# Weight sums of the value product made in two column pieces, and copies of projected V shared by two engines

## Chip, cores and metric

The kernel runs on one core of one Trainium2 chip. The metric is the device time of one execution in microseconds, the median over several runs; lower is better.

## What is computed

The reference is a linear attention followed by a gated feed-forward layer, for 8 batches, 8 heads, 1024 positions and a head width of 64:

```python
k_proj = np.einsum('ks,bhsd->bhkd', E, k)          # 64 projected keys per head
v_proj = np.einsum('ks,bhsd->bhkd', F, v)
scores = scale * np.matmul(q, k_proj.transpose(0, 1, 3, 2))
attn = softmax(scores)                              # over the 64 projected keys
x = np.matmul(attn, v_proj)                         # laid out as 8192 tokens x 512
gate = 1.0 / (1.0 + np.exp(-(x @ w_gate)))          # 512 x 1536
out = (gate * (x @ w_val)) @ w_out                  # w_val 512 x 1536, w_out 1536 x 512
```

## The kernel before

The tokens are worked in blocks of 512 columns, two blocks for each batch, sixteen in all. For a block, the gate product (G), the value product (V), the gating and the output product follow each other, and the attention of a later batch is laid between them. All operations are added to one plan in program order (class `Plan`); each engine runs its own operations in that order, and a wait is put in front of an operation for each semaphore value that its inputs, or the buffers that it overwrites, still need. So the order in which the program calls its helpers is the order of every engine's queue. Lists called `todo` give the slots of that order, and `put(i, fn)` or `on(u, j, fn)` adds a piece of work behind slot i, or behind slot 11 + 9u + j.

Block 0 is worked plainly: `mstep(0, m)` multiplies the m-th of twelve 128-column chunks of both weights, and `gate` (L1126) reads the V bank on VectorE. From block 1 on, V is made with Strassen's method in Winograd's form: seven products of half size in place of eight. A unit K is a block and a "quad" q (K = 3 x block + q); a quad is two chunks of the first half of the 1536 columns with the two that lie 768 columns on. `v_pieces` (L1497) issues the seven products of a unit in five steps, in the order p1, p26, p57, p4, p3, with the four gate steps `g_step` of the unit between them. They accumulate in two PSUM banks, called a and c in the code. ScalarE takes snapshots of bank a (`v_snap`, L1465), VectorE adds bank c to a snapshot (`v_add`, L1468), and `hidden` (L1444) multiplies with the gate. The first step p57 starts a new sum in bank c, so it waits for the `v_add(0)` of p26, which reads bank c.

The products take sums of the inputs and sums of the weights. The sums of the inputs, S1 to S4, are made per block by `xs_sums` (L1406, VectorE, 128 x 512 bf16 each). The sums of the weights, T1 to T4, are made once, by `vt_sums` (L1372 to L1394, VectorE, 128 x 1536 bf16 each): T3 = B22 - B12, T2 = T3 + B11, T4 = B21 - T2, and T1 = B12 - B11, which overwrites B12. T2, T3 and T4 go to the tensor `vT`, T1 stays in `wV`. Each sum covers all three quads. T2 is used by p26, T1 and T3 by p57, T4 by p4.

Around the start of block 1 (K = 3, its first unit) VectorE's queue reads: gate of chunk 10 of block 0; T3; S1; S2; gate of chunk 11; T2; T1; S3; S4; T4; `v_add(0)`; `hidden`. The gate of chunk 11 frees the PSUM bank that p26 takes as its bank c. In unit K = 4 the function `v_alone` (L811) turns the projected keys of batch 1 and projects its values into one PSUM bank; `keep_v` (L529) copies four quarters (64 x 256) of that bank to `vpD`, all four on ScalarE; ScalarE's next item is `v_snap(2)`, for which the PE's next product p4 waits. The four copies read one bank, and the plan lets operations on one bank follow one another.

The loads come through two queues. POOL issues (L282), in this order, the second batch's Q, K and V, then the output weights `wO` behind the first two DMA transposes of Q (SP, L745), then K, V and Q of batch 2. The output products of block 0 (`oproj`, L1146) are the first to use `wO`.

Of the kernel before, what the change touches and what calls it, by code (L numbers as in the profile page):

```python
# [12 lines left out]
P = 128  # L13
# [5 lines left out]
DFF = 1536  # L19
# [99 lines left out]
def bass_linformer_attn__then__ffn_glu_sigmoid_kernel(  # L119
# [11 lines left out]
    B = q.shape[0]  # L131
# [6 lines left out]
    with contextlib.ExitStack() as es:  # L138

        def sbuf(name, shape, dtype):  # L140
            return es.enter_context(nc.sbuf_tensor(name, shape, dtype))


        vT = sbuf("vT", [P, 3, 2, DFF // 2], BF16)
# [61 lines left out]
        wV = sbuf("wV", [P, NI, DFF], BF16)  # L206
# [49 lines left out]
        def mm(b, o, lhsT, rhs, r, start=True, stop=True, tp=None, tr=False, read=False):  # L256
            kw = {"skip_group_check": True} if read else {}
            if tp is not None:
                kw["tile_position"] = tp
            if tr:  # L260
                kw["is_transpose"] = True
            else:
                kw["start"], kw["stop"] = start, stop
            return add("PE", lambda e: e.matmul(o, lhsT, rhs, **kw), r=r, x=[("bank", b)])  # L264

        def act(o, i, r, w, b=None, func=AF.Copy, scale=1.0):
            x = [] if b is None else [("bank", b)]
            return add("ACT", lambda e: e.activation(o, i, func, scale=scale), r=r, w=w, x=x)  # L268

        def dve(fn, r, w, b=None):  # L270
            x = [] if b is None else [("bank", b)]
            return add("DVE", fn, r=r, w=w, x=x)
# [224 lines left out]
        def pairs(R):  # L497
            return slice(0, NR) if R is None else slice(2 * R, 2 * R + 2)

        def both(R):  # L500
            return (0, 1) if R is None else (R,)

        def project(n, w, bks, c0, R=None):
            src = KV[n][:, :, :].rearrange("p (r h) (t d) -> p h t r d", h=2, t=NT)
            width = 256 if R is None else 128
            for t in range(NT):
                for h in range(2):
                    mm(
                        bks[h],
                        bank[bks[h]][64 * h : 64 * h + 64, c0 : c0 + width],  # L510
                        EFT[:, t, 64 * w : 64 * w + 64],
                        src[:, h, t, pairs(R), :],
                        [("KV", n, x) for x in both(R)] + [("EFT", t // 4)],
                        start=(t == 0),
                        stop=(t == NT - 1),
                        tp=(0, 64 * h),
                    )
# [11 lines left out]
        def keep_v(bks, c0, engines, R=None):  # L529
            vv = vpD[:, :, :].rearrange("p (r h) d -> p r h d", h=2)  # L530
            width = 256 if R is None else 128
            for n, (h, g) in enumerate(((0, 0), (1, 1), (0, 1), (1, 0))):
                o = vv[64 * g : 64 * g + 64, pairs(R), h, :]
                i = bank[bks[h]][64 * h : 64 * h + 64, c0 : c0 + width].rearrange(
                    "p (r d) -> p r d", d=DH
                )
                ws = [("vpD", h, g, x) for x in both(R)]
                if engines[n] == "ACT":
                    act(o, i, [], ws, b=bks[h])
                else:  # L540
                    dve(lambda e, o=o, i=i: e.tensor_copy(o, i), [], ws, b=bks[h])

        def turn_k(ring, R=None):
            bk = ring.next()
            ob = bank[bk][:, :].bitcast(BF16)
            rs = range(NR)[pairs(R)]
            for n, r in enumerate(rs):
                for g in range(2):
                    mm(
                        bk,  # L550
                        ob[64 * g : 64 * g + 64, n * P : (n + 1) * P],
                        kp[:, r, :],
                        ident[:, :],
                        [("kp", r // 2), "ident"],
                        tr=True,
                        tp=(0, 64 * g),
                    )
            act(
                kpD[:, 2 * rs[0] : 2 * rs[-1] + 2, :].rearrange("p h c -> p (h c)"),
                ob[:, 0 : P * len(rs)],  # L560
                [],
                [("kpD", x) for x in both(R)],
                b=bk,
            )
# [236 lines left out]
        def attention(b):  # L801
# [9 lines left out]
            def v_alone():  # L811
                bk = AA.take()
                turn_k(Ring((bk,)))
                AA.append(bk)
                bk = AA.take()
                project(1, 1, [bk, bk], 0)
                keep_v([bk, bk], 0, ["ACT"] * 4)
                AA.append(bk)

            def sc_one(r, bks):  # L820
# [234 lines left out]
            def keep_kv(n):  # L1055
# [15 lines left out]
                mul=mul,  # L1071
                k_alone=k_alone,
                v_alone=v_alone,
                bc=bc,
            )
# [4 lines left out]
        def chunk(m):  # L1080
            return max(x for x in range(len(WCH) - 1) if WCH[x] <= m * P)
# [101 lines left out]
        H6 = NF // 2  # L1183
# [185 lines left out]

        def vt_sums(n):  # L1372
            B11, B12 = wV[:, 0:2, 0 : DFF // 2], wV[:, 0:2, DFF // 2 : DFF]
            B21, B22 = wV[:, 2:4, 0 : DFF // 2], wV[:, 2:4, DFF // 2 : DFF]
            o, a, b = {
                3: (vT[:, 1, :, :], B22, B12),
                1: (B12, B12, B11),
                2: (vT[:, 0, :, :], vT[:, 1, :, :], B11),
                4: (vT[:, 2, :, :], B21, vT[:, 0, :, :]),
            }[n]  # L1380
            w = [("vT", n)]
            if n == 1:
                w += [("wV", j, 0) for j in (3, 4, 5)]
            else:
                w += ["bsel8f", "identf", "count", "pats"]
            r = [("wV", j, x) for j in range(6) for x in range(2)]
            if n == 1:
                r = [("wV", j, 0) for j in range(3)]
            if n == 2:
                r.append(("vT", 3))  # L1390
            if n == 4:
                r = [("wV", j, 1) for j in range(3)] + [("vT", 2)]
            op = ALU.add if n == 2 else ALU.subtract
            dve(lambda e: e.tensor_tensor(o, a, b, op), r, w)  # L1394

        def x_part(blk, n):
            s, hf = blk // 2 % 2, blk % 2
            if n[0] == "S":
                return xS[blk % 2][:, int(n[1]) - 1, :, :], [("xS", blk % 2, int(n[1]))]
            tok, i0 = int(n[1]) - 1, 2 * (n[2] == "2")  # L1400
            return (
                xT[s][:, i0 : i0 + 2, hf, 256 * tok : 256 * tok + 256],
                [("xT", s, i0 + i, hf, tok) for i in range(2)],
            )
# [11 lines left out]
        def v_product(blk, q, bk, A, B, start=False, stop=False):  # L1416
            x, kx = x_part(blk, A)
            for j in range(2):
                for i in range(2):
                    m = 2 * q + j  # L1420
                    if B in ("T2", "T3", "T4"):
                        w, kw = vT[:, int(B[1]) - 2, i, m * P : (m + 1) * P], ("vT", int(B[1]))
                    else:
                        if B == "T1":
                            ii, mm_, kw = i, m + H6, ("vT", 1)
                        else:
                            ii, mm_ = i + 2 * (B[1] == "2"), m + H6 * (B[2] == "2")
                            kw = ("wV", chunk(mm_), ii // 2)
                        w = wV[:, ii, mm_ * P : (mm_ + 1) * P]
                    mm(  # L1430
                        bk,
                        bank[bk][:, 256 * j : 256 * j + 256],
                        w,
                        x[:, i, :],
                        kx + [kw],
                        start=start and i == 0 and j == 0,
                        stop=stop and i == 1 and j == 1,
                        read=True,
                    )
# [161 lines left out]
        def put(i, fn):  # L1601
            at.setdefault(i, []).append(fn)
# [4 lines left out]
        def x_sums(blk, *ns):  # L1607
            return lambda: [xs_sums(blk, n) for n in ns]
# [8 lines left out]
        put(4, second_loads)  # L1617
        put(6, lambda: (den2(), xo2(0), xo2(1)))
        put(8, lambda: (bc2(0)(), bc2(1)()))
        put(9, lambda: vt_sums(3))  # L1620
        put(9, x_sums(1, 1, 2))
        put(10, lambda: (vt_sums(2), vt_sums(1)))

        def own_banks():
            FF[:] = [ffn.next() for _ in range(4)]
# [25 lines left out]
        def on(u, j, fn):  # L1651
            put(11 + 9 * u + j, fn)

        on(0, 1, x_sums(1, 3, 4))
        on(0, 2, lambda: vt_sums(4))
        n1 = attention(1)
        late1 = n1["late"]
        on(0, 6, n1["k_alone"])
# [39 lines left out]
        for b in range(1, B):  # L1698
# [37 lines left out]
            if b + 1 < B:  # L1736
                n = attention(b + 1)
# [80 lines left out]
```

The softmax here doesn't subtract the row's maximum and nothing guards it: scores larger than these inputs give would overflow.

## Time and profile before

| | |
|---|---|
| median of 9 runs | 534.79 us (533.49 to 534.95) |
| the profiled execution's own time | 534.55 us |
| span of its profile | 532.8 us |
| PE (matmul) busy | 519.7 us, 98% of the span |
| VectorE (DVE) busy | 415.0 us, 78% |
| ScalarE (ACT) busy | 307.8 us, 58% |
| GpSimd (POOL) busy | 133.6 us, 25% |

The span is the time from the first to the last recorded instruction. In a timeline a line gives the start in us, the busy time, the engine, the line of the code and the operation with its tensors; "x4" are four instructions merged, and the bracket tells how long the engine had been idle before and what ended that. Most operations are recorded by a helper and so all have one line, L264 for a matmul and L268 for a ScalarE operation; they are told apart by their tensors. `pF` are the PSUM banks of the feed-forward part and `pA` those of the attention. PE is the matmul, PEld the load of its weights.

### The profile page before, as it was taken

How to read it: one execution, taken by the hardware profiler on the slowest of the kernel's cores; microseconds unless marked ns; L12 is line 12 of the kernel's file. 1: busy time of each engine (PE TensorE's matmuls, PEld its weight loads, DVE VectorE, ACT ScalarE, POOL GpSimd, SP SyncE). 2: the span in 40 equal slices, each digit the busy share in tenths (PEclk: the TensorE clock that was granted, in tenths of full speed). 3: DMA queues.
4: the chain of work that ended last, by engine and by line, in shares of the span. 5: the costliest groups of instructions: out<-in, count | busy, mean ns of one | idle time of the engine just before them, and what ended most of it. 6: DMA issues, size and time to landing. Idle time of an engine off the chain costs nothing.

```text
span 532.8 us, 10476 instructions
## 1 busy us (share of the span) xinstructions
PE 519.7 (98%) x4173; PEld 351.1 (66%) x4173; DVE 415.0 (78%) x675; ACT 307.8 (58%) x553; POOL 133.6 (25%) x148
## 2 busy tenths in 40 slices
PE   5998999999999999999999999999999999999997
PEld 4544545766757667585766757676685767677676
DVE  3548588678987788867988689887898788987855
ACT  2554682597375574846658474664738564554641
POOL 9310200104810076000940039100650008300000
PEclk9999999999999999999999999999999999999999
DMA  9999998893295243922469213972520020202022
GB/s 165 200 199 203 136 206 179 174 209 58 43 217 97 81 91 47 233 39 83 89 124 194 80 32 62 193 123 80 77 80 18 0 82 3 81 0 80 1 81 79
DMA packets 77153, 56.18 MB, mean 105 GB/s; under 512 B 34800, under 2 KB 69296, under 8 KB 77104
## 3 DMA queue, kind: packets, MB, share of 16 engines
q0 software_dynamic: 33984, 29.89, 36.4%
q1 hardware_dynamic: 43120, 25.63, 19.1%
q8 instruction: 32, 0.52, 0.4%
q14 instruction: 17, 0.14, 0.1%
HBM read 60.29 MB, written 16.78 MB: 145 GB/s over the span
## 4 chain that ended last, share of the span: by engine, by line
PE 93%; DMA 2%; DVE 2%; POOL 1%; ACT 1%; issue 1%; DVEq 0%; POOLq 0%
PE pF L264 61%; PE pA L264 32%; DMA KVs<-in_v_dram 2%; DVE vT L1394 0%; DVE hT L1133 0%; DVE vsnap L1471 0%; ACT vsnap L268 0%; POOL KVs L282 0%; DVE xT L691 0%; ACT vpD L268 0%; POOL Qb L282 0%; DVE xS L1414 0%; DVE rden L639 0%; DVE ost L1338 0%; POOL quad L356 0%
## 5 line engine op out<-in xcount | busy, mean ns | idle before, releaser
L264 PE MATMUL pF<-xT,wG 128*128 128x512 bf16 x768 | 197.5, 379 | 0.3
L926 POOL PARTITION_BROADCAST KVs<-eT x96 | 97.0, 1036 | 243.6 <-PE pF L264 149.4
L268 ACT ACTIVATE sig<-pF 128x512 f32<-128x512 f32 x192 | 115.4, 601 | 49.2 <-PE pF L264 47.0
L1471 DVE TENSOR_TENSOR vsnap<-pF,vsnap 128x512 f32<-128x512 f32 x135 | 93.0, 689 | 44.3 <-PE pF L264 31.0
L264 PEld LDWEIGHTS pF<-xT,wG 128*128 128x128 bf16 x768 | 74.2, 98 | 54.4 <-issue 1.7
L268 ACT ACTIVATE vsnap<-pF 128x512 f32<-128x512 f32 x135 | 80.7, 598 | 49.0 <-PE pF L264 46.0
L1452 DVE SCALAR_TENSOR_TENSOR hT<-sig,vsnap 128x512 bf16<-128x512 f32 x135 | 93.5, 693 | 6.2
L264 PE MATMUL pF<-xT,wV 128*128 128x256 bf16 (+1 forms) x408 | 66.9, 286 | 0.0
L264 PE MATMUL pA<-wO,hT 128*128 128x256 bf16 x534 | 63.4, 273 | 0.0
L264 PEld LDWEIGHTS pA<-wO,hT 128*128 128x128 bf16 x534 | 52.1, 98 | 6.6 <-DVE ost L1267 0.3
L264 PE MATMUL pF<-xS,wV 128*128 128x256 bf16 x360 | 54.1, 273 | 1.8 <-DVE vsnap L1471 1.5
L264 PE MATMUL pF<-xS,vT 128*128 128x256 bf16 x360 | 54.0, 273 | 0.3 <-DVE vT L1394 0.3
L264 PEld LDWEIGHTS pF<-xT,wV 128*128 128x128 bf16 x408 | 38.2, 98 | 24.0 <-issue 5.7
L264 PEld LDWEIGHTS pF<-xS,wV 128*128 128x128 bf16 x360 | 34.3, 98 | 27.2 <-DVE vsnap L1471 6.5
L958 DVE TENSOR_TENSOR xT<-xu,KVs 128x512 bf16<-128x512 f32 x48 | 47.4, 1023 | 1.2 <-POOL KVs L926 0.7
L268 ACT ACTIVATE EF<-pA 128x512 f32<-128x512 f32 x30 | 17.9, 597 | 46.9 <-PE pA L264 46.9
L264 PE MATMUL pA<-wT,hT 128*128 128x256 bf16 x360 | 44.2, 273 | 0.0
L264 PE MATMUL pA<-wT,hS 128*128 128x256 bf16 x360 | 41.8, 273 | 0.0
L264 PEld LDWEIGHTS pA<-wT,hT 128*128 128x128 bf16 x360 | 35.1, 98 | 7.4 <-ACT snap L268 0.3
L264 PEld LDWEIGHTS pF<-xS,vT 128*128 128x128 bf16 x360 | 35.1, 98 | 4.6 <-DVE vT L1394 0.5
L264 PEld LDWEIGHTS pA<-wT,hS 128*128 128x128 bf16 x360 | 35.2, 98 | 4.3 <-issue 0.2
L1267 DVE SCALAR_TENSOR_TENSOR ost<-pA,EF 128x512 f32<-128x512 f32 x29 | 20.0, 688 | 19.8 <-PE pA L264 19.7
(113 smaller groups left out, 487.4 us busy)
## 6 DMA issues: line engine op xcount, KB each, us to landing
out_dram<-ost SPq DMA_DIRECT2D x60, 256.0 KB, 2.4
Qb<-in_q_dram POOLq DMA_DIRECT2D x7, 1024.0 KB, 20.3
KVs<-in_k_dram POOLq DMA_DIRECT2D x7, 1024.0 KB, 12.2
KVs<-in_v_dram POOLq DMA_DIRECT2D x7, 1024.0 KB, 16.1
wO<-in_moe_w_out_dram POOLq DMA_DIRECT2D x1, 1536.0 KB, 12.6
wG<-in_moe_w_gate_dram POOLq DMA_DIRECT2D x5, 256.0 KB, 18.3
wV<-in_moe_w_val_dram POOLq DMA_DIRECT2D x5, 256.0 KB, 18.9
KVs<-in_k_dram POOLq DMA_DIRECT2D x2, 512.0 KB, 9.2
```

The source lines that it names most:

```text
L264: return add("PE", lambda e: e.matmul(o, lhsT, rhs, **kw), r=r, x=[("bank", b)])
L268: return add("ACT", lambda e: e.activation(o, i, func, scale=scale), r=r, w=w, x=x)
L926: lambda e, n=n, i=2 * rnd + c, j=j, parts=parts: e.partition_broadcast(rb[0:parts, n, :], rrow[32 * j : 32 * j + 1, i, :], channels=parts),
L958: lambda e: e.tensor_tensor(xT[s][:, r, :, 256 * g : 256 * g + 256], xu[:, n, :].rearrange("p (f c) -> p f c", f=2), y.rearrange("p (f c) ...
L1267: lambda e: e.scalar_tensor_tensor(o, bank[bk][:, :].rearrange("p (j c) -> p j c", j=2), 0.5, snap[n].rearrange("p (j c) -> p j c", j=2), ...
L1452: lambda e: e.scalar_tensor_tensor(o, sg[:, :, cc], 1.0, x.rearrange("p (j c) -> p j c", j=2), ALU.add, ALU.mult,),
L1471: lambda e: e.tensor_tensor(o, bank[bk][:, :], o, ALU.add),
```

## The change

`vt_sums` gets a second argument, the piece. Piece 0 holds columns 0 to 255 of each half, which is what the first quad of a block uses; piece 1 holds columns 256 to 767, for the other two quads. Each of the four sums is now two instructions, of 128 x 2 x 256 and 128 x 2 x 512 elements, and the keys by which the plan orders readers and writers name the piece. T3 and T2 of piece 0 are made before the gate of chunk 11, behind S1 and S2; T1 of piece 0 is made behind that gate, then S3, then T4 of piece 0. S4 and the four sums of piece 1 are placed behind the first `v_add` and `hidden` of unit K = 3, between the later steps of that unit. In `v_alone`, the second and the fourth copy of projected V go from ScalarE to VectorE. The order of the PE's instructions, and the orders of SP and POOL, stay as they are.

```diff
--- before.py
+++ after.py
@@ -814,7 +814,7 @@
                 AA.append(bk)
                 bk = AA.take()
                 project(1, 1, [bk, bk], 0)
-                keep_v([bk, bk], 0, ["ACT"] * 4)
+                keep_v([bk, bk], 0, ["ACT", "DVE", "ACT", "DVE"])
                 AA.append(bk)
 
             def sc_one(r, bks):
@@ -1369,27 +1369,32 @@
 
 
 
-        def vt_sums(n):
-            B11, B12 = wV[:, 0:2, 0 : DFF // 2], wV[:, 0:2, DFF // 2 : DFF]
-            B21, B22 = wV[:, 2:4, 0 : DFF // 2], wV[:, 2:4, DFF // 2 : DFF]
+        def vt_sums(n, part):
+            c0, c1 = ((0, 256), (256, DFF // 2))[part]
+            js = ((0,), (1, 2))[part]
+            B11 = wV[:, 0:2, c0:c1]
+            B12 = wV[:, 0:2, DFF // 2 + c0 : DFF // 2 + c1]
+            B21 = wV[:, 2:4, c0:c1]
+            B22 = wV[:, 2:4, DFF // 2 + c0 : DFF // 2 + c1]
+            T = [vT[:, k, :, c0:c1] for k in range(3)]
             o, a, b = {
-                3: (vT[:, 1, :, :], B22, B12),
+                3: (T[1], B22, B12),
                 1: (B12, B12, B11),
-                2: (vT[:, 0, :, :], vT[:, 1, :, :], B11),
-                4: (vT[:, 2, :, :], B21, vT[:, 0, :, :]),
+                2: (T[0], T[1], B11),
+                4: (T[2], B21, T[0]),
             }[n]
-            w = [("vT", n)]
+            w = [("vT", n, part)]
             if n == 1:
-                w += [("wV", j, 0) for j in (3, 4, 5)]
+                w += [("wV", 3 + j, 0) for j in js]
             else:
                 w += ["bsel8f", "identf", "count", "pats"]
-            r = [("wV", j, x) for j in range(6) for x in range(2)]
+            r = [("wV", j + k, x) for j in js for k in (0, 3) for x in range(2)]
             if n == 1:
-                r = [("wV", j, 0) for j in range(3)]
+                r = [("wV", j, 0) for j in js]
             if n == 2:
-                r.append(("vT", 3))
+                r = [("wV", j, 0) for j in js] + [("vT", 3, part)]
             if n == 4:
-                r = [("wV", j, 1) for j in range(3)] + [("vT", 2)]
+                r = [("wV", j, 1) for j in js] + [("vT", 2, part)]
             op = ALU.add if n == 2 else ALU.subtract
             dve(lambda e: e.tensor_tensor(o, a, b, op), r, w)
 
@@ -1419,10 +1424,10 @@
                 for i in range(2):
                     m = 2 * q + j
                     if B in ("T2", "T3", "T4"):
-                        w, kw = vT[:, int(B[1]) - 2, i, m * P : (m + 1) * P], ("vT", int(B[1]))
+                        w, kw = vT[:, int(B[1]) - 2, i, m * P : (m + 1) * P], ("vT", int(B[1]), int(m > 1))
                     else:
                         if B == "T1":
-                            ii, mm_, kw = i, m + H6, ("vT", 1)
+                            ii, mm_, kw = i, m + H6, ("vT", 1, int(m > 1))
                         else:
                             ii, mm_ = i + 2 * (B[1] == "2"), m + H6 * (B[2] == "2")
                             kw = ("wV", chunk(mm_), ii // 2)
@@ -1617,9 +1622,9 @@
         put(4, second_loads)
         put(6, lambda: (den2(), xo2(0), xo2(1)))
         put(8, lambda: (bc2(0)(), bc2(1)()))
-        put(9, lambda: vt_sums(3))
         put(9, x_sums(1, 1, 2))
-        put(10, lambda: (vt_sums(2), vt_sums(1)))
+        put(9, lambda: (vt_sums(3, 0), vt_sums(2, 0)))
+        put(10, lambda: vt_sums(1, 0))
 
         def own_banks():
             FF[:] = [ffn.next() for _ in range(4)]
@@ -1651,8 +1656,13 @@
         def on(u, j, fn):
             put(11 + 9 * u + j, fn)
 
-        on(0, 1, x_sums(1, 3, 4))
-        on(0, 2, lambda: vt_sums(4))
+        on(0, 1, x_sums(1, 3))
+        on(0, 2, lambda: vt_sums(4, 0))
+        on(0, 3, x_sums(1, 4))
+        on(0, 3, lambda: vt_sums(3, 1))
+        on(0, 4, lambda: vt_sums(2, 1))
+        on(0, 5, lambda: vt_sums(1, 1))
+        on(0, 7, lambda: vt_sums(4, 1))
         n1 = attention(1)
         late1 = n1["late"]
         on(0, 6, n1["k_alone"])
```

## Prediction

> **What bounds the kernel now.** I read the page's busy times first, then the windows (busy time of each engine in stretches), then the timeline of each engine where the PE idles.
>
> ```profile
> PE 519.7 (98%) x4173; PEld 351.1 (66%) x4173; DVE 415.0 (78%) x675; ACT 307.8 (58%) x553; POOL 133.6 (25%) x148
> ```
> ```profile
> 49.50:56.00 6.50, 4.97 (x42) 3.08 (x43) 4.34 (x8) 2.78 (x5) 0.00 (x0) 1.00 1.28 150
> 62.00:68.00 6.00, 5.51 (x43) 2.95 (x42) 3.95 (x6) 4.61 (x10) 2.01 (x3) 1.00 1.19 180
> 85.00:516.00 431.00, 430.72 (x3388) 298.60 (x3387) 350.70 (x548) 258.49 (x460) 109.75 (x111) 1.00 0.43 88
> ```
>
> The columns are the stretch, its length, then busy time (and instructions) of PE, PEld, DVE, ACT, POOL, the clock and the DMA share. From 85 to 516 us the PE is never free: nothing done there by another engine can help, and what is won before 85 us is kept to the end. The start of block 1 (49.5 to 56) holds 1.5 us of PE idle, and 62 to 68 another 0.5. The timeline shows where:
>
> ```profile
> 49.43 0.61 PE L264 MATMUL pF<-xS,vT 128*128 128x256 bf16 x4 [0.26 <-DVE vT L1394]
> 49.87 1.03 PE L264 MATMUL pF<-xT,wG 128*128 128x512 bf16 x4
> 52.43 0.61 PE L264 MATMUL pF<-xS,wV 128*128 128x256 bf16 x4 [1.53 <-DVE vsnap L1471]
> ...
> 63.77 0.61 PE L264 MATMUL pF<-xT,vT 128*128 128x256 bf16 x4 [0.49 <-ACT vsnap L268]
> ```
> ```profile
> 46.16 0.95 DVE L1394 TENSOR_TENSOR vT<-wV 128x1536 bf16<-128x1536 bf16 x1
> 47.02 0.42 DVE L1414 TENSOR_TENSOR xS<-xT 128x512 bf16<-128x512 bf16 x1
> 47.48 0.42 DVE L1414 TENSOR_TENSOR xS<-xS,xT 128x512 bf16<-128x512 bf16 x1
> 47.82 0.68 DVE L1133 SCALAR_TENSOR_TENSOR hT<-sig,pF 128x512 bf16<-128x512 f32 x1
> 48.42 0.95 DVE L1394 TENSOR_TENSOR vT<-vT,wV 128x1536 bf16<-128x1536 bf16 x1
> 49.29 0.95 DVE L1394 TENSOR_TENSOR wV<-wV 128x1536 bf16<-128x1536 bf16 x1
> ...
> 50.83 0.95 DVE L1394 TENSOR_TENSOR vT<-wV,vT 128x1536 bf16<-128x1536 bf16 x1
> 51.70 0.68 DVE L1471 TENSOR_TENSOR vsnap<-pF,vsnap 128x512 f32<-128x512 f32 x1
> ```
>
> p57 (52.43) waits for `v_add(0)` at 51.70. That add had its inputs long before (the PE finished them at 49.17, ScalarE its snapshot at 48.41); it stands behind the four long sums on a DVE with no gap. The wait at 63.77 is p4 of K = 4, behind a ScalarE snapshot that stands behind four copies:
>
> ```profile
> 61.50 1.59 ACT L268 ACTIVATE vpD<-pA 64x256 bf16<-64x256 f32 x4 [0.16 <-PE pA L264]
> 63.12 0.60 ACT L268 ACTIVATE vsnap<-pF 128x512 f32<-128x512 f32 x1
> ```
>
> What comes due next is the output weights, whose first user is at 73.33:
>
> ```profile
> 58.43 1.01 POOL L282 DMA_DIRECT2D wO<-in_moe_w_out_dram  x1 [23.14 <-DMA qT<-Qb]
> ```
> ```profile
> 73.33 2.76 PE L264 MATMUL pF<-wO,hT 128*128 128x512 bf16 x12
> ```
> ```profile
> wO<-in_moe_w_out_dram POOLq DMA_DIRECT2D x1, 1536.0 KB, 12.6
> ```
>
> **What the Trainium skill says.** "VectorE: DVE Perf Modes", section "Side-by-side: where the cycles go for N=2048 bf16": a bf16 tensor_tensor gives two results a cycle and pays about 150 cycles once per instruction, so I estimate (512/2 + 158)/0.96 = 431 ns for a 512-element sum. The trace agrees: 420 ns at 512, 684 to 690 at 1024, 949 at 1536. "Perfetto Trace Analysis", section "Optimizing Scalar/DVE Operations": where these engines aren't saturated but cause bubbles on others, breaking up instructions may let work finish sooner. That is this case: DVE is 78% busy. "PSUM — Partial Sum Buffer", section "PSUM bank collisions raise a hardware error ⚠️": two engines must not touch one bank and quadrant at once. So the four copies cannot run side by side, and the plan indeed makes each wait for the one before; no run here shows a collision. "DMA: Bandwidth & Descriptors", section "Queues, rings and completion order": each DMA engine takes turns between its queues, so an earlier store takes bandwidth from a load; used in the rivals.
>
> **The change, part by part.** Pitch is the distance of two starts on an engine. From the DVE rows: 0.87 at 1536 elements, 0.60 at 1024 (70.41 to the next), 0.34 at 512 (50.16 to 50.49), and 0.12 more where an instruction reads the result of the one before (47.02 to 47.48).
>
> Sums, added cost: four pieces of 0.34 and four of 0.60 are 3.76 us for 3.48 before, and 0.24 for T2 now standing right behind T3 twice: 0.5 us more DVE time. DVE has gaps of 0.97, 1.08 and 3.23 us in front of 54.15, 55.92 and 63.75, which take it; without them it would come on the adds.
>
> Sums, p26: S1 at 46.16, S2 46.62, T3 46.96, T2 47.42, gate of chunk 11 at 47.76 (47.82 before). It ends at 48.44 and p26 starts at 48.50 (48.56 before). T2 is done by then, so its second product follows at 48.94 and not 49.43; the gate step g2 starts at 49.38 and leaves the PE free at 50.24 (0.87 for four 512-column matmuls).
>
> Sums, p57: behind the gate (pitch 0.60) T1 at 48.36, S3 48.70, T4 49.04, `v_add(0)` at 49.38 to 50.06. So p57 can start when the PE is free, at 50.25: **2.18 us earlier** than 52.43. What is late next? S3·T3 needs S3 (done 49.12) and the second snapshot (about 50.2): it runs at 50.7. K of batch 1 landed at 33.53 + 16.2 = 49.7, before its use at 52.1. p4 at 53.1 needs T4, done.
>
> Sums, piece 1: `hidden` 50.16, S4 50.76, T3 51.10, T2 51.82, `v_add(2)` 52.42 to 53.11 (needed by p3 at 54.4), T1 53.0, `hidden` 53.75 and 54.35, T4 54.95, `v_add(1)` 55.55 to 56.24, `hidden` 56.27. Behind them wait the banks: the gate step of K = 4 at 57.01 takes the bank of `v_add(1)`, with 0.77 us to spare. The pieces themselves are used from 56.6 on. So piece 1 costs nothing, with that cover.
>
> Copies: on the clock of before, ScalarE copies at 61.50 (0.38), DVE at 61.92, ScalarE at 62.38, and the snapshot starts at 62.80 in place of 63.12; the fourth copy runs beside it. A DVE copy of 64 x 128 takes 0.294 in the trace; 128 elements more, at one a cycle of 0.96 GHz ("VectorE: DVE Perf Modes", section "Specifications", an estimate), make 0.294 + 0.133 = 0.43; a handoff 0.03 (snapshot end 63.72, add 63.75). p4 starts at 63.45: **0.32 us**. Bounds: 0 if the handoffs cost 0.1 more each, 0.65 if p4 stops waiting. DVE is idle there; the queue behind its waiting copy is `v_add(2)`, which needs the snapshot anyway.
>
> Sum: 2.18 + 0.32 = 2.50, so the PE reaches the output products at 73.33 - 2.50 = 70.83. But `wO` lands at 58.43 + 12.6 = 71.03. Its issue waits for transposes of Q and nothing of the change, so it doesn't move. With up to 0.1 for the signal the output products start at about 71.1, **2.25 us earlier**. 0.25 of the gain is lost to this new wait; most of the copies' gain goes there.
>
> After that: V of batch 2 lands at 62.24 + 20.7 = 82.9; its use moves from 86.08 to 83.83. Q of batch 2 lands at 89.1, its transposes move from 91.37 to about 89.2, first use at 102.5. Both hold, so 2.25 us reaches the end.
>
> Against the profiled execution: span 532.8 - 2.25 = 530.55, own time 534.55 - 2.25 = 532.3. The median was 0.24 above that execution: 534.79 - 2.25 = **532.5**.
>
> **The rivals.** (1) The DMA takes more of it: `wO` lands up to 1 us later, or V of batch 2 does. The stores of block 0 start 2.25 us earlier and take their turns before V has landed; the second store now starts at 78.4 and not 80.65, so about 0.6 of its 256 KB more can go ahead of V: at 207 GB/s, the rate in that stretch, 0.75 us against a slack of 0.9. For it: DMA share over 1 until 86 us. Against it: 0.9 covers it. Price up to 1 us: 533.5.
>
> (2) The pieces, which read and write rows with gaps, run at one element a cycle, the slow mode of the section quoted first: 0.53 us more for each large piece, 0.27 for each small. `v_add(0)` ends at 51.13, p57 starts at 51.2, `v_add(1)` ends at 59.3 and K = 4's gate step starts at 59.35 (59.19 before), so the split's gain is gone; the copies' 0.32 stays: 534.6. Against it: the S sums read such rows too and take 420 ns.
>
> (3) Slower: the same mechanism, dearer. With d more per large piece (half for small), `v_add(1)` ends at 56.3 + 6d against 59.19, so the total changes by 6d - 3.2: slower from d = 0.54 on, and 1.3 us slower (536.1) at d = 0.75, a piece of 1.35 us. Against it: no bf16 sum of this size in the trace passes 0.69.
>
> (4) That the change doesn't do what it says: the add at 51.70 waits for PE and ScalarE by its semaphores, and if one of these were late and not the queue, the split would win nothing and only the copies' 0.3 remain: 534.5. Against it: both were done by 49.2, and the chain of waits runs through T3, T2, T4 and `v_add(0)`.
>
> **How the numbers follow.** Forecast 0.77 (531.9 to 533.0: copies and signal at their bounds, 0.3 for scatter, most runs shown lying within 0.3 of their median), (1) 0.10, (2) and (4) together 0.08, (3) 0.05. The range reaches into (1): 531.7 to 533.5. About 0.2%, 1.07 us, is what a measurement can tell from no change: faster 0.77 + 0.08 = 0.85, same 0.09, slower 0.06.
>
> **What would show it.** p57 of K = 3 at about 50.25 with no wait for an add; sums of 0.42 and 0.69; ScalarE's snapshot in K = 4 behind two copies; and a wait of some 0.25 us for the `wO` load at about 71.1. Wrong if p57 still waits past 51, if a bank is late in K = 4, or if the later wait is much longer.

## Result and profile after

| | before | changed |
|---|---|---|
| median | 534.55 us (29 runs) | 532.45 us (9 runs) |
| ratio, 95% interval | | 0.9962 (0.9953 to 0.9972) |

The ratio makes 2.0 us (1.5 to 2.5). The forecast was 532.5 us, 2.25 us below the median of before that it started from (534.79 us, 9 runs). The profiled execution of the changed kernel, which is not one of the nine, took 537.72 us over a span of 535.9: its PE clock was granted at 0.92 and 0.84 in the two stretches up to 43 us, and everything behind them came 4.9 to 5.7 us later than in its profiles at full clock. So its stages are read by the distances within them, and a second profile of the same kernel, at full clock, stands beside it (run `e1_again`, span 529.9 us).

The page of the changed kernel, busy times and clock row:

```profile
PE 522.9 (98%) x4173; PEld 353.1 (66%) x4173; DVE 416.3 (78%) x681; ACT 307.1 (57%) x551; POOL 133.4 (25%) x148
...
PEclk9699999999999999999999999999999999999999
```

The windows of the profile at full clock (columns as in the prediction):

```profile
49.50:56.00 6.50, 6.50 (x54) 4.21 (x53) 6.31 (x12) 3.73 (x8) 0.00 (x0) 1.00 1.35 174
56.00:62.00 6.00, 5.85 (x55) 3.71 (x54) 3.88 (x7) 4.09 (x8) 2.43 (x3) 1.00 1.11 141
62.00:68.00 6.00, 6.00 (x49) 3.63 (x48) 5.19 (x9) 5.16 (x10) 1.22 (x2) 1.00 1.19 178
```

The stretch that held 1.53 us of PE idle holds none, and DVE is nearly full in it (6.31 of 6.50 in place of 4.34): the second pieces of the sums now run there, beside PE work. The rest of a wait, 0.15, is left in the next stretch; it is p4's wait for its snapshot (`e1_fourth` names it: 0.15, ACT vsnap). In the timelines of the changed kernel, first the PE: p26 and p57 of K = 3, p4 of K = 4, the first output product.

```profile
53.28 0.61 PE L264 MATMUL pF<-xT,wV 128*128 128x256 bf16 x4
...
55.03 0.60 PE L264 MATMUL pF<-xS,wV 128*128 128x256 bf16 x4
...
66.01 0.61 PE L264 MATMUL pF<-xT,vT 128*128 128x256 bf16 x4
...
75.58 2.76 PE L264 MATMUL pF<-wO,hT 128*128 128x512 bf16 x12
```

p57 comes 1.75 us behind p26 and has no bracket: it waits for nobody. Before, it was 3.87 us (48.56 to 52.43). Then DVE, with the small pieces ahead of the add at 54.15, the large ones behind it, and the two copies:

```profile
51.75 0.42 DVE L1399 TENSOR_TENSOR vT<-wV 128x512 bf16<-128x512 bf16 x1
52.20 0.42 DVE L1399 TENSOR_TENSOR vT<-vT,wV 128x512 bf16<-128x512 bf16 x1
52.54 0.68 DVE L1133 SCALAR_TENSOR_TENSOR hT<-sig,pF 128x512 bf16<-128x512 f32 x1
53.14 0.42 DVE L1399 TENSOR_TENSOR wV<-wV 128x512 bf16<-128x512 bf16 x1
53.48 0.42 DVE L1419 TENSOR_TENSOR xS<-xT 128x512 bf16<-128x512 bf16 x1
53.81 0.42 DVE L1399 TENSOR_TENSOR vT<-wV,vT 128x512 bf16<-128x512 bf16 x1
54.15 0.68 DVE L1476 TENSOR_TENSOR vsnap<-pF,vsnap 128x512 f32<-128x512 f32 x1
...
55.88 0.69 DVE L1399 TENSOR_TENSOR vT<-wV 128x1024 bf16<-128x1024 bf16 x1
56.60 0.69 DVE L1399 TENSOR_TENSOR vT<-vT,wV 128x1024 bf16<-128x1024 bf16 x1
...
59.71 0.69 DVE L1399 TENSOR_TENSOR vT<-wV,vT 128x1024 bf16<-128x1024 bf16 x1
60.31 0.68 DVE L1476 TENSOR_TENSOR vsnap<-pF,vsnap 128x512 f32<-128x512 f32 x1
...
64.50 0.43 DVE L541 CAST vpD<-pA 64x256 bf16<-64x256 f32 x1 [1.38 <-ACT vpD L268]
```

And ScalarE, where the snapshot stands behind two copies:

```profile
64.09 0.38 ACT L268 ACTIVATE vpD<-pA 64x256 bf16<-64x256 f32 x1 [0.16 <-PE pA L264]
64.96 0.38 ACT L268 ACTIVATE vpD<-pA 64x256 bf16<-64x256 f32 x1 [0.49 <-DVE vpD L541]
65.36 0.60 ACT L268 ACTIVATE vsnap<-pF 128x512 f32<-128x512 f32 x1
```

From the first copy to the snapshot is 1.27 us; before, it was 1.62 (61.50 to 63.12).

### The profile page after: what moved, and what is told of

It reads as the page before. It is cut to its first block, busy times and chain, and to the rows that moved or that the text cites. A ratio compares the mean times of both kernels' runs of the same rounds, so it can differ in the third digit from the quotient of the medians.

```text
span 535.9 us, 10478 instructions
## 1 busy us (share of the span) xinstructions
PE 522.9 (98%) x4173; PEld 353.1 (66%) x4173; DVE 416.3 (78%) x681; ACT 307.1 (57%) x551; POOL 133.4 (25%) x148
## 4 chain that ended last, share of the span: by engine, by line
PE 95%; DMA 3%; POOL 1%; ACT 0%; DVE 0%; issue 0%; POOLq 0%
PE pF L264 63%; PE pA L264 32%; DMA KVs<-in_v_dram 3%; ACT vsnap L268 0%; POOL KVs L282 0%; POOL Qb L282 0%; DVE vsnap L1476 0%; ACT vpD L268 0%; DVE vpD L541 0%; DVE ost L1338 0%; POOL quad L356 0%; POOLq L1813 0%
## 6 DMA issues: line engine op xcount, KB each, us to landing
wO<-in_moe_w_out_dram POOLq DMA_DIRECT2D x1, 1536.0 KB, 12.4
```

## How the runs are compared

The first 45 us of an execution vary: the load of Q of the second batch (batch 1) was issued anywhere from 31.16 to 32.84 us in the profiles at full clock. From the first output product to the end, the three full-clock profiles of the changed kernel take 459.45 to 459.51 us, the kernel before 459.47. So the change is decided between these two, and the table measures from the start of p26 of K = 3 (PE timeline of each run). In the kernel before this is the line

```profile
48.56 0.61 PE L264 MATMUL pF<-xT,wV 128*128 128x256 bf16 x4
```

The table leaves out that p26 itself follows the gate step in front of it 0.08 us sooner after the change (47.51 to 48.56 before, 47.13 to 48.10 in `e1_again`).

| run | p57 | p4 of K = 4 | output products | ratio to before (interval) |
|---|---|---|---|---|
| before | 3.87 | 15.21 | 24.77 | 1 |
| changed (`e1_again`) | 1.75 | 12.73 | 22.29 | 0.9966 (0.9955 to 0.9977) |
| changed (`e1_third`) | 1.74 | 12.72 | 22.29 | 0.9957 (0.9941 to 0.9973) |
| changed (`e1_fourth`) | 1.74 | 12.73 | 22.58 | 0.9959 (0.9943 to 0.9974) |
| sums only | 1.74 | 13.07 | 22.80 | 0.9966 (0.9955 to 0.9978) |
| copies only | 3.88 | 14.87 | 24.43 | 0.9998 (0.9990 to 1.0007) |
| order and copies (`e5_order_only`) | 2.67 | 13.66 | 23.43 | 0.9978 (0.9964 to 0.9992) |
| order alone | 2.68 | 14.01 | 23.57 | 0.9971 (0.9956 to 0.9986) |
| more sums | 1.74 | 13.59 | 23.15 | 0.9979 (0.9961 to 0.9997) |
| `wO` earlier, first and second | 1.74 | 12.72, 12.73 | 22.29, 22.29 | 0.9948 (0.9936 to 0.9960), 0.9954 (0.9937 to 0.9971) |
| copies later, first and second | 1.75 | 12.41, 12.42 | 21.97, 21.97 | 0.9952 (0.9935 to 0.9968), 0.9954 (0.9937 to 0.9970) |

Where one kernel ran more than once, the distances repeat to 0.01 us, but for the output products of `e1_fourth`, which waited for a load (below); the ratios carry the scatter of the first 45 us and of the load.

## Experiments

**The changed kernel at full clock**, three times.

> The changed kernel as it is, for a profile at full clock. Theory (the load of the output weights takes back what the copies win): p57 of K = 3 starts at 50.25, p4 of K = 4 at 61.2, the output products wait some 0.3 us for the load and start at 71.1, 2.25 us earlier than in the kernel before, and the whole is 2.2 us faster (ratio 0.9958). Rival (the load is early enough): no wait there, the output products start at 70.8, and the whole is 2.5 us faster (0.9953).

> The changed kernel again, beside the next three. Theory: in those executions in which the load of the output weights lands late against the PE, the output products wait for it; the time is 1.8 to 2.3 us below that of the kernel before (ratio 0.9957 to 0.9966). Rival (the load never binds): the 2.56 us that the PE has won by the output products show in full, ratio 0.9952.

> The changed kernel once more, to set beside the next two on one chip. Within one execution the PE should be 2.5 us ahead of the kernel before at the output products, unless the load of the output weights lands less than 22.3 us after p26 of K = 3 starts. Theory (that load binds in part of the executions): median 1.8 to 2.3 us below the kernel before. Rival: 2.5.

p57 and p4 came at the distances that were expected. The wait for the load of the output weights was absent in the first two and there in the third. So the first run missed its expectation: it had no wait, as its rival said, and its ratio (0.9966, or 1.8 us) is neither the 2.2 us of the theory nor the 2.5 of the rival. In the third the trace names the wait (PE, then POOL's issue, then the load's time from issue to landing):

```profile
70.15 2.75 PE L264 MATMUL pF<-wO,hT 128*128 128x512 bf16 x12 [0.23 <-DMA wO<-in_moe_w_out_dram]
```
```profile
57.06 1.01 POOL L282 DMA_DIRECT2D wO<-in_moe_w_out_dram  x1 [22.67 <-DMA qT<-Qb]
```
```profile
wO<-in_moe_w_out_dram POOLq DMA_DIRECT2D x1, 1536.0 KB, 13.0
```

It landed at 57.06 + 13.0 = 70.06; the PE was ready at 47.57 + 22.29 = 69.86 and started at 70.15, 0.29 later. In the other two it landed at 57.54 + 12.4 = 69.94 and 57.80 + 12.4 = 70.20, the PE was ready at 70.39 and 70.63. So the wait is real, and binds in part of the executions: one of these three, and two of the variants below.

**Each half alone.** Sums only:

```diff
-                keep_v([bk, bk], 0, ["ACT", "DVE", "ACT", "DVE"])
+                keep_v([bk, bk], 0, ["ACT"] * 4)
```

> Only the sums in two pieces; the four copies of projected V all on ScalarE as before. Theory: p57 of K = 3 at 50.25, 2.18 us won; p4 of K = 4 still waits 0.5 behind the copies; the output products would be ready at 71.15, which is when the load is there, so 2.15 us faster (ratio 0.996), within 0.1 of the whole change. Rival (no load wait in the whole change): 0.3 to 0.4 us slower than the whole change.

Copies only is the kernel before with the opposite edit.

> Only the copies shared by two engines; the sums whole as before. Both theories: p4 of K = 4 at 63.4 in place of 63.77, the output products at 73.0, after the load has landed, so 0.35 us faster (ratio 0.9993). Rival (the handoffs cost as much as the parallel work wins): no difference, and p4 at 63.8.

With the sums only, p57 is where the whole change has it, and p4 has its old wait (p4 of K = 4 on the PE):

```profile
60.85 0.61 PE L264 MATMUL pF<-xT,vT 128*128 128x256 bf16 x4 [0.49 <-ACT vsnap L268]
```

From p57 to p4 it takes 11.33 us with four ScalarE copies, 10.98 with two: 0.35 for the copies. With the copies only it is 10.99 against 11.34, the same 0.35, and the 0.34 is still there at the output products. So the two halves act apart from each other. The total of the copies alone could not be told from no change (interval 0.9990 to 1.0007, which holds the 0.9993 expected). For the sums only, the total is that of the whole change within the intervals, and its output products started 0.17 us later than its p4 allows (13.07 + 9.56 = 22.63, measured 22.80): its load landed at 57.74 + 12.7 = 70.44 and the product started at 70.58. The trace gives this wait to a VectorE operation that had ended 0.4 us before; the times point to the load. The run with order and copies below shows the same: 23.22 by its p4, measured 23.43, its load landed at 57.28 + 13.2 = 70.48 and the product started at 70.61.

**Order or size.** The kernel before with whole sums, only placed differently:

```diff
-        on(0, 1, x_sums(1, 3, 4))
-        on(0, 2, lambda: vt_sums(4))
+        on(0, 1, x_sums(1, 3))
+        on(0, 3, x_sums(1, 4))
+        on(0, 3, lambda: vt_sums(4))
```

> The kernel before with whole sums, but T4 and S4 placed behind the first add and hidden of K = 3, as the change places S4; copies on ScalarE. Theory (the queue in front of the add is the cause): the add starts at 50.50 and p57 at 51.24, 1.2 us earlier than 52.43; T4 is done at 53.2, before p4 at 54.1; 1.2 us faster (ratio 0.9978). The other 1.0 us of the change is then the smaller pieces. Rival (only smaller pieces help, the order does nothing): no difference.

The kernel that ran under this name also had the copies shared, against what its expectation says; the last run of the study is the one without.

> The kernel before with whole sums and the four copies on ScalarE; only T4 and S4 are placed behind the first add and hidden of K = 3. Theory (the queue in front of the add): the add some 1.2 us earlier, p57 2.68 us behind p26 in place of 3.87, the total 1.2 us below the kernel before (0.9978). Rival (the order does nothing without smaller pieces): 3.87 stays.

In the order alone, p26, p57 and p4 on the PE, and the add on DVE:

```profile
47.37 0.61 PE L264 MATMUL pF<-xT,wV 128*128 128x256 bf16 x4
...
50.05 0.61 PE L264 MATMUL pF<-xS,wV 128*128 128x256 bf16 x4 [0.33 <-DVE vsnap L1471]
...
61.38 0.61 PE L264 MATMUL pF<-xT,vT 128*128 128x256 bf16 x4 [0.49 <-ACT vsnap L268]
```
```profile
49.31 0.68 DVE L1471 TENSOR_TENSOR vsnap<-pF,vsnap 128x512 f32<-128x512 f32 x1
```

p57 is 2.68 behind p26, as expected to the digit, and a wait of 0.33 for the add stays. So 1.19 of the 2.13 us that p57 wins come from moving T4 and S4 behind the add, which needs no smaller piece. The other 0.94 come with the pieces, but not by their size alone. The add is 1.94 us behind p26 here and 0.87 in the changed kernel; by the pitches, 0.87 of this is T2, which now stands in front of the gate of chunk 11, 0.53 is the smaller T1, and T4 of piece 0 takes 0.34 back. No run separates the place of T2 from the size; by the same pitches a whole T2 in that place would hold up the gate, and with it p26, by 0.9 us or more.

**The cover of the second pieces.** Three spare sums of the same size were put behind T3, T2 and T4 of the second piece; their results go to unused room and nothing of the computation is left out.

```diff
-        on(0, 3, lambda: vt_sums(3, 1))
+        on(0, 3, lambda: (vt_sums(3, 1), spare(1)))
-        on(0, 4, lambda: vt_sums(2, 1))
+        on(0, 4, lambda: (vt_sums(2, 1), spare(2)))
-        on(0, 7, lambda: vt_sums(4, 1))
+        on(0, 7, lambda: (vt_sums(4, 1), spare(3)))
```

> The changed kernel with three spare sums of 128 x 1024 bf16, one behind each of the second pieces of T3, T2 and T4; their results are used by nothing. Theory (the second pieces are covered by 0.77 us in front of the gate step of K = 4 and by no more): the spare 1.8 us bring the third add of K = 3 from 55.55 to 57.1, and the gate step of K = 4 waits 0.8 us for its bank; of that 0.5 to 0.8 stay in the total. Rival (VectorE has room there): no difference to the changed kernel.

The third add of K = 3 in this run's DVE timeline, the gate step of K = 4 that waits for it, and what the PE's weight loads waited for between 44 and 75 us (us in total, times, longest):

```profile
56.71 0.68 DVE L1481 TENSOR_TENSOR vsnap<-pF,vsnap 128x512 f32<-128x512 f32 x1
```
```profile
57.45 1.04 PE L264 MATMUL pF<-xT,wG 128*128 128x512 bf16 x4 [0.50 <-DVE vsnap L1481]
```
```profile
PEld pF L264 <- DVE vsnap L1481: 1.5, 4, 0.8
```

In the changed kernel the last row (`e1_third`) and the add and the gate step (`e1_again`, whose p26 starts at 48.10 as in this run) read:

```profile
PEld pF L264 <- DVE vsnap L1476: 0.6, 2, 0.4
```
```profile
55.13 0.68 DVE L1476 TENSOR_TENSOR vsnap<-pF,vsnap 128x512 f32<-128x512 f32 x1
```
```profile
56.59 1.03 PE L264 MATMUL pF<-xT,wG 128*128 128x512 bf16 x4
```

The add is 8.61 us behind p26; 8.6 was expected (57.1 less 48.5). It comes 1.58 us later than in the changed kernel, and the gate step 0.86: the other 0.72 is the cover, and the rest of the 1.8 us of spare work went into gaps and waits that DVE had there. Two more waits for an add appear, and p4 and the output products are 0.86 us later too. The total rose by 1.2 us in the ratios (0.9979 against 0.9957), more than the 0.5 to 0.8 expected, but the intervals overlap. From the first output product to the end this run's profile took 462.25 us, 2.8 more than the 459.5 of the kernel before and of `e1_third`, and nothing here explains that; so the distance in the trace is the firmer number, and the size of the effect on the total stays open. The rival, that VectorE has room for the spare sums, falls.

**The load earlier.** The load of the output weights waits for one transpose in place of two:

```diff
-                r=turned()[:2],
+                r=turned()[:1],
```

> The changed kernel with the load of the output weights waiting for one transpose of Q in place of two, so that it is issued some 2 us earlier. Theory (the load takes back part of the gain): 0.2 to 0.6 us faster than the changed kernel, and no wait in front of the output products. Rival: no difference to the changed kernel.

> The earlier load of the output weights again. Theory (the load binds in part of the executions of the changed kernel): 0.2 to 0.6 us faster than the changed kernel of this call, 2.4 to 2.6 below the kernel before. Rival (it never binds): the same as the changed kernel.

The issue in the first of the two runs, and its output products:

```profile
55.08 1.01 POOL L282 DMA_DIRECT2D wO<-in_moe_w_out_dram  x1 [21.29 <-DMA qT<-Qb]
```
```profile
69.28 2.76 PE L264 MATMUL pF<-wO,hT 128*128 128x512 bf16 x12
```

It landed at 55.08 + 12.8 = 67.88, 1.4 us ahead of its use, in the run whose p26 came earliest of all (46.99); the distance stays 22.29. 0.2 to 0.6 us of gain was expected both times. Against the changed kernel measured beside it, the first run was 0.5 us faster (531.17 against 531.71) and the second 0.1 slower (531.75 against 531.63), with overlapping intervals both times. That the load binds in some executions is shown; how much of the median it costs isn't.

**The copies behind p57 of K = 4**, with the earlier load:

```diff
-        on(1, 4, n1["v_alone"])
+        on(1, 5, n1["v_alone"])
```

> As the run with the earlier load of the output weights, and besides, the projection of V and its four copies follow p57 of K = 4 in place of going ahead of it, so that the last snapshot of K = 4 stands in front of the copies on ScalarE. Theory (the snapshot queued behind the copies is what p4 of K = 4 still waits for): no wait there, 0.25 us faster than with the earlier load alone. Rival (the second copy on VectorE now holds up the multiplication behind it and with it a bank): no gain, a new wait at the scores of batch 1.

> The earlier load and the copies behind p57 of K = 4 again. The trace showed the output products 21.97 us after p26 of K = 3, and 22.29 with the earlier load alone: 0.3 us faster than the run with the earlier load alone, 2.8 below the kernel before. Rival: no difference to it that can be measured.

p4 and the output products of the first of these:

```profile
60.67 0.60 PE L264 MATMUL pF<-xT,vT 128*128 128x256 bf16 x4
...
70.23 2.76 PE L264 MATMUL pF<-wO,hT 128*128 128x512 bf16 x12
```

Both come 0.32 us earlier than with the earlier load alone, in both runs, so the snapshot behind the copies was what p4 still waited for, and no bank was late. In the medians it doesn't show: 0.25 to 0.3 us of gain over the earlier load alone was expected, and they are 0.25 and 0.14 us higher (531.42 against 531.17, 531.89 against 531.75), within the scatter. Both versions are faster than the kernel before; that either beats the changed kernel in total is not shown.

## Why the prediction was right

**p26 and p57.** The sum of queue pitches held: p57 came 1.75 us behind p26, the distance that was forecast (48.50 to 50.25), and the add 0.87 behind it (0.88 forecast). Small pieces took 0.42 and large ones 0.69 us, so the rivals of a slow mode, (2) and (3), fall: the rows with gaps cost nothing. The queue of long sums in front of the add was the cause, and rival (4) falls, as the order alone shows: with T4 and S4 out of that queue, the add came 1.20 us earlier against p26 and p57 1.19.

**The second pieces.** They cost nothing, with the cover forecast: the third add was due 7.05 us behind p26 and came at 7.03 (`e1_again`, 55.13 less 48.10). With the add 1.58 us later, the gate step came 0.86 later; so the cover was 0.72 where 0.77 was forecast.

**The copies.** 0.35 us, 0.32 forecast. The DVE copy took the estimated 0.43 and the handoffs between the engines about 0.03. But the prediction's conclusion that the four copies cannot run side by side doesn't follow from what it draws on, the Trainium skill's page "PSUM — Partial Sum Buffer", section "PSUM bank collisions raise a hardware error ⚠️": that section allows two engines in one bank if they are in different quadrants, and a quadrant there is 32 partitions. In the code, the copies are not of four quarters of the bank but of two halves, each copied twice: the first and third, on ScalarE, read partitions 0 to 63, the second and fourth, on VectorE, partitions 64 to 127. What puts them one behind the other is the plan, which keeps one key for a whole bank. No run here lets them overlap, so what that would give is not shown; placing them behind p57 of K = 4 wins 0.32 us at p4, as the last experiment shows.

**The load of the output weights.** This step was half right. The PE did win 2.5 us up to the output products (24.77 to 22.29, and 0.08 up to p26), and the load does come due there next. But "it doesn't move" took one execution's landing time for a fixed one. Its landing was 71.03 in the profile that I read and 69.94 to 70.20 in three others, and p26 itself started at 47.57 to 48.34; the margin between them ran from +0.45 to -0.20 us. So a loss like the forecast 0.25 is one case (0.29 in `e1_fourth`) and none the other. By the traces the total should be 2.25 to 2.5 us; measured were 2.0 (1.5 to 2.5). No run settles the remainder, which is of the size of the scatter: the order alone, worth 1.2 us in its trace, measured 1.5.

**The number.** That 532.45 was measured where 532.5 was forecast is in part luck. The gain was 2.0 and not 2.25 us, and the median of before, over 29 runs, lay 0.24 below the one that the forecast started from; the two nearly cancel.

**Two slips that don't bear on the forecast.** The pitch of 0.60 at 1024 elements stands in the trace of before between 69.81 and 70.41; behind 70.41 it is 0.72. And rival (2)'s `v_add(1)` would end at 59.44 by its own costs (56.24, four times 0.53 and four times 0.27), not at 59.3, so its price was some 0.15 us too low.

**After that.** The tail of 459.5 us is the same in both kernels, so V and Q of batch 2 were in time, and rival (1) didn't come about in the profiles.

## What to carry to other kernels

Where the PE waits for a short operation that had its inputs long before, look at what stands in front of it in its engine's queue, and first move what isn't due: here that gave 1.19 of the 2.13 us of p57 without a new instruction. Cut the sums by who needs which part first, and compute which buffer release behind the later parts becomes the next to be late. When a gain brings an engine up to a load, read the load's landing in several executions, against the engine and not against the span's start, before taking it for a fixed time.

## What was not expected of the hardware

In the trace of before, four ScalarE copies of 64 x 256 started 0.40 us apart at 0.38 each, and two of 64 x 512 took 1.21 together at 0.59 each (from 89.11), so they didn't overlap, while 128 x 512 operations of 0.60 start 0.49 apart (67.09 and 67.58). The plan puts no wait between two ScalarE operations for sharing a bank, so a wait of the program is not the reason. Whether it is the 64 partitions, the bank that they share, or that one copy starts at other partitions than the one before, no run shows. And the start varies: with one program at full clock, p26 of K = 3 began between 47.57 and 48.34 us, more than twice what the copies are worth; so the small parts were read from the distances and not from the medians.
